# DeltaNet and Fourier mixing on one core: odd heads' tokens of batches 2 to 4 with their partition halves exchanged

## The chip, the cores and the metric

The kernel runs on one core of a Trainium2 chip. The metric is the device time of one execution in microseconds (us); lower is better. Engines are named as in the profile: PE is the matrix engine (PEld its weight loads), DVE the vector engine, ACT the scalar engine, POOL the third elementwise engine, SP the queue that issues most transfers. Matrix results land in eight banks of an accumulator memory, PSUM, from where DVE or ACT must copy them out.

## The reference, cut to what matters

Four batches, eight heads, 768 tokens, head size 48. First a recurrence per head, then a block that mixes over all tokens and features by Fourier transforms, and a two-layer network.

```python
for t in range(S):                      # DeltaNet, per batch and head
    y[:, :, t] = np.einsum('bhd,bhde->bhe', q[:, :, t], state)
    v_old = np.einsum('bhde,bhd->bhe', state, kt)
    state = state + bt * np.einsum('bhd,bhe->bhde', kt, vt - v_old)
...
x = y.transpose(0, 2, 1, 3).reshape(B, S, H * D)
mixed = np.real(np.fft.fft(np.fft.fft(x, axis=1), axis=2))
u = x + mixed
un = (u - mu) / np.sqrt(var + 1e-06)
out = u + np.maximum(un @ w_ch1, 0.0) @ w_ch2
```

Keys are divided by their norms first.

## The kernel before, in words

The 768 tokens of a batch are cut into six units of 128 tokens, so there are units 0 to 23; a unit stands on the 128 partitions as two chunks `c` of 64 tokens. Heads are taken in four pairs `j`, with `s` = 0 for the even and 1 for the odd head of a pair. Within a chunk the recurrence is solved as a triangular system (products of keys in `gram`, an inverse built on DVE in `invert`, lines 859 and 864, and joined by small products in `quarters`); from chunk to chunk only the state `st` (48 x 48 for each head) is carried.

For a unit of batches 2 to 4 (units 6 to 23) these steps follow each other:

- `load`: k, q and v by one transfer each, or two of 121 and 7 rows for units 6 to 13 (line 399, queue of SP).
- `ahead`: the inverse times v gives U (tile `ut`, buffers `u`), copied out of PSUM in three parts; the inverse times k gives the factor for the state.
- `step(z, c)`: sixteen small products of the state (PE, `f1`: U's correction and the outputs' first part); two subtractions on 64 partitions from U, one for the even and one for the odd heads (DVE, line 1174); two copies of outputs to `x` (ACT or DVE); eight products of keys and U (PE, `f2`); one addition to the state on 128 partitions (DVE, line 1203). The next `f1` waits for that state.
- `outputs`: sixteen products, and four additions on 64 partitions to `x` (DVE, line 1240), or two copies and two additions in the first unit of a batch.

The odd head's result of chunk `c` comes out of PE on the other 64 partitions than the even head's, and this is why the subtractions and additions go by 64 partitions. Batch 1 (units 0 to 5) takes another path (`chain0`, `outputs0`), which the change leaves alone.

After the last unit of a batch come its mixing (`folds` on DVE, `seq6` and `feat` on PE) and the network (`mlp`, `mlpw`: groups of four or six wide matrix products, first layer and second layer in turn). Their products stand between the steps of the next batch's recurrence.

Each instruction belongs to an operation `P.op`; the order of all operations, the engine of those that two engines can do, the PSUM banks, and a few products that only keep PE running (`fill`, lines 2057 and 2063) are written out as the text ORDER. Each engine takes its instructions in that order and waits at each for what it reads.

Of the kernel before, what the change touches and what calls it, by code (L numbers as in the profile page):

```python
# [53 lines left out]
APBAAAWAZAZAXv8AABAaAaAOBA+A+AIBAFBAGBAJBA9A9AHBANBACBA7A7ADBAMDA8A8AQDALDAEDAKDARATAYAbBCAeDEAdBAcC  # L54
AUFASAfBAgBAhGHH-H-AVCxCxAwAiDXDXBSABIIIIAjBPCDH3H3Alv+EAkBQCC6C6AmBTCv+FDFDFBRCAvA-ECBUCBCAFBACBVDB
BBCv-EBDCBWBkA1Axv-EAyBECAzBFCAA5BXA0A2v-EAtBZBGBYAnv-EA3BvBHv-EBwBaBJv-EBzAoBIBev-EB0BKArv-EB3BOBjv
-EBhBbv-EDgBhBcv-EBMIAIAv-EIHIHB4v-EA6BlC5AtB7ApBpv-EBmDODOAqwAFB8BNDCBUBnBLB-BoBfIQIQCACyBACDBiH4H4
BtDYGHCEBdv-EBqDfDfC0CDaCC7FCIXIXCHCzCBrDGDACIDZCBsDhHBBxCLDHCv-EByCMDICIPIPB1CPDbGDDjCB2CQDiCB5C1AB
CTC8CB6C9CCUv-EB9DdCIoIoCXB+C3Cv-ECYCBAuv-ECbIJCCIYIYCcDkHFCFA4AsCGBgCfDPCDCJCgC2CDuDuCKv-EIBCjCkCNC
+BACnDDCIfIfv-ECOv-ECov-EDQCv-EDNBLCpC-Cv-EILDJCBCRDRCDyInInv-ED1CD2BESDzCCSD3DDcCD0BCrDLCEXGETCDwDw  # L60
D4CIDv-ECVCqD5BEYCEVCH5DSDGDWBvCWv-EEWCD7EUCCZv-EDACD6CaDlCD8EZBCdIRD9H6EAADTCCeEbD+CEav+EChEcD-CCiE
dEDCICEBCEgHClEeBEECCmECCv-EH8EhCCsEFDH7v-EBuIKEGCv-ECtH9DmCEHCv-EEkCv-EEJCCuFCCv-EDKCEICv-EFACEjBEN
BAEfCH+IZEKFCE+FqIwIwFBCDEBEiCv-EIxIxEPCE-BFDDFuBELCIEIyIyEOCFvHCwITIvIvIFEQFFECEMCv-ECvFwCERCElDFtC
DUCFFCIGFrCGZCEwEnCFsBEoCGWI6I6DMEmCFxHEpCI5I5GbGDVEyCI7I7GYCHFCEqDBFHI8I8GXCFzEzCHCFyDoDoC4IzExHAHD
BEsCFGErCFIHHCI0I1E0FJIMGcCFMBHICHEBI2E1Cv-EGaBDpBFNCGdDFLCFQBI3EtGCF0FPCF1I9E5GfNmFPGeEuBFOCF4DIgIg
ISE6CI4EvCE7CE2DqCFKBJIJIHGBIUFRBJGJGI+E8JHJHIaF3CFUBIVwAEJEJEE3CF8BFTCGgJFJFF5BE9CHJGF2CF7BJDJDF6BI
NFcIhFVBHLF9DHKFSCFfBI-FeBFWGBF+BIbGhFdAHJAF-CE4BJBGACFYBFgGBCHMGjCGkCFXBIjFhBGCBDObHNGmCHPBFlHOCIiG
DCHQGFnBFmCGECDBJJFoIOFZBDFpCJCHTCv-EJcJcGnCGIFaCJbJbIpGlBIkv-EJdJdFbCHRBGKCFiJaJaGLCJKHUCGoBJQJQGiC
DrBGJAHIrNnE4IcNoFdDsBFkCGMJLJeJeJMGpCHSBNlE5GNCJNGFDGJZJZGqBFjBGrCGRNpGXGHBGsCHVBGGCIlNsE9GSBGTCGtC
v-EN-GqHWBGUHXCGOHZCJOGVBIdJmJmHYBGQBJfG0DvDvGPBGuCBNxFxG2CIWJnJnJhG1GDOAGHGvBGwCG3CImNyNyJSJSG4DnJo  # L70
JoHaABIqG5CDtDtGxCHJRJRHbBG9GyBGzCHcCIsG6DeG+CG-CItHAG8BG7COBABHBBKqHgKpv-EHjCODBHdCHHiCIuHhDGRZODHe
COCCOdHfBIeHkONHhHmJPJPKrHlBRNFiKtHpOOKrKsHnCNzBAHoCJqJqKwHrCHqBKxN0CKyHsKzOECHHtCRQHqKuN1CK2NrFQHxK
vDxDxK6HuBFJTJlJlHyBK5RMRMK0HvCN2ADJUHzCJpJpHwCJVK1RRK0K9H0LAK3N5LLEGJgH1CK4H2CLBOFK7N4JiRnOFN7K8OIN
qDeLELUBFK-K+RPHzLCLIRYKtLDLHR0N4LMLGLFRSRSLJJWRULULVLKJrOHJXN3N8OJN6LNJsN9JYLWLOCLSBJjLRBJzJzOGLQCR
1OGRaADLaBLXCwACOKRbCLdGCJkLPCRcCN+J-J-LbCOPHAOMLeOLJ0J0LmEDLgJxJxORCLfJ+J+LhOQCLvFCJ9J9JuLTCLiJyJyL
nLcCOSGAKAKALpLZCLoNvFgLYCLjJtLqRdHDJ7J7LkJ8J8LrOXJvLwLlOTL4EBLsOURjReMTLtRhOVRiMUCLuOYL5MKDGMWMVCL7
OWL6J1MXBOaMBCAJwMYCKBJ2MbEKLKLOZKKKKKDKCLyKMKMLxNwF6KEMCJ3OcNuFWKFKHKHMLMZBRmK3KJKJSCKIKIKGOeOfJ4Kh
# [11 lines left out]
MtYtYOTfDBRJYXNREYLYYYMRISPCYbTgRLTiYZThBYaRKYWYfGDT7HAYgBYhCTkCTjCUABT8DGTlYPTmBCYNT9CUBBNSCYiFDTnT
pToCYdT+CUXATqCYjTrEYmYnTtBGUYCTsT-CUCCATvTwTuUZEYqUGCNTHBUECUbBYoUdCYlUaCUcBYkUFUDTxU2UHDYpUeEFYcUI  # L90
YsUfACUkCUiCUJGDUgCNWUhCbiUhU3YuX9StUKYvX+SuUNCYwULCbcYfYxUMUjCU4U6YyNUEU5U9YzY1Y6U+UOANVCUQCGUPbdYw
U7UlDFbvYxUTY7bjEAUUURNXGU8blCUSUoUnCbkCUmVAU-Y8VDUqCVBVGbmADY9beU-UrVCNkNkUsECbpNZVFUwCY+brY-NYCUvZ
# [153 lines left out]
def kernel(  # L246
# [895 lines left out]
    def step(z, c, pr):  # L1142
# [8 lines left out]
        for i in range(k):  # L1151
# [36 lines left out]
            if n == 2 * NT - 1:  # L1188
                continue
# [907 lines left out]
```

## Time and profile before

| what | value |
|---|---|
| three runs, median | 633.43 us (630.84 to 637.3) |
| the profiled execution | 633.59 us, span of its instructions 631.8 us |
| granted PE clock, mean | 0.997 |
| PE instructions | 9694 matmul records for 5078 products of the program |
| DVE, ACT instructions | 1597, 890 |

A row of the groups reads: line, engine, operation, result <- operands, shape, count | busy us, mean ns of one | idle time of the engine just before, and what ended it. One small product leaves two records on PE, so a count of 1056 is 528 products. PE's busy time counts the modelled ends of products, so a short wait can lie under it unseen.

### The profile page before, as it was taken

The page shows a single profiled execution, that of the slowest core. Times are in us where ns is not written, and L with a number is a line of the kernel's source. Part 1 is how long each engine was busy: PE and PEld are TensorE (multiplying, and loading weights), DVE is VectorE, ACT ScalarE, POOL GpSimd, SP SyncE. Part 2 cuts the span into 40 slices and gives each one's busy share as a digit, 9 for nine tenths or more (in the row PEclk, how much of TensorE's full clock was granted, in tenths as well). Part 3 has the DMA queues.
Part 4 walks back from the last instruction along what each step waited for, and adds up shares of the span by engine and source line. Part 5 has one row for each costly group of instructions (what it writes and reads, how often), then busy time and mean ns, then how long its engine had stood idle before and what let it go on. Part 6 is the DMA issues. An engine that isn't in the chain of part 4 may idle for free.

```text
span 631.8 us, 22692 instructions
## 1 busy us (share of the span) xinstructions
PE 613.7 (97%) x9694; PEld 508.3 (80%) x9694; DVE 530.8 (84%) x1597; ACT 287.5 (46%) x890; POOL 31.0 (5%) x37
## 2 busy tenths in 40 slices
PE   9999899999999899999999999999999999999997
PEld 8788798777678678877787778867778789999997
DVE  6999799999997799999957999999865867777563
ACT  6999657633556435447443334553631112222111
POOL 2013302210000000000000000000000000000000
PEclk9999899999999999999999999999999999999999
DMA  8842654500014151000330330000000000010100
GB/s 191 225 136 74 161 132 113 141 1 1 3 29 104 38 124 22 2 1 3 66 78 23 87 71 1 2 28 2 4 3 2 2 1 1 1 51 1 51 26 25
DMA packets 85442, 31.99 MB, mean 51 GB/s; under 512 B 75996, under 2 KB 80829, under 8 KB 85341
## 3 DMA queue, kind: packets, MB, share of 16 engines
q1 hardware_dynamic: 85149, 30.31, 19.6%
q8 instruction: 76, 1.25, 0.8%
q10 hardware_dynamic: 192, 0.23, 0.2%
q14 instruction: 25, 0.20, 0.1%
HBM read 25.82 MB, written 4.72 MB: 48 GB/s over the span
## 4 chain that ended last, share of the span: by engine, by line
PE 46%; DVE 3%; issue 1%; ACT 0%; DVEq 0%
PE pp L348 44%; PE pp L351 1%; DVE tmp L859 1%; DVE rr L864 1%; DVE gd L876 0%; DVE st L1203 0%; DVE u L1174 0%; ACT us L357 0%; DVE x L1787 0%; DVE x L359 0%; DVE rr L873 0%; DVE x L1240 0%; DVE us L1728 0%; DVE us L1580 0%; DVE u L1787 0%
## 5 line engine op out<-in xcount | busy, mean ns | idle before, releaser
L348 PE MATMUL pp<-R,w 128*128 128x256 f32 (+1 forms) x832 | 180.6, 366 | 0.2 <-ACT R L357 0.2
L348 PEld LDWEIGHTS pp<-R,w 128*128 128x128 f32 x832 | 146.2, 190 | 20.3 <-ACT R L357 0.4
L348 PE MATMUL pp<-w,R 128*128 128x384 f32 x384 | 133.9, 493 | 0.0
L357 ACT ACTIVATE us<-pp 32x128 f32<-32x128 f32 (+3 forms) x218 | 71.3, 352 | 78.0 <-PE pp L348 47.9
L348 PEld LDWEIGHTS pp<-w,R 128*128 128x128 f32 x384 | 70.2, 190 | 40.6
L348 PE MATMUL pp<-us 64*64 64x64 f32 (+4 forms) x2784 | 69.3, 230 | 0.7 <-ACT u L357 0.4
L348 PEld LDWEIGHTS pp<-us 64*64 64x64 f32 (+2 forms) x2784 | 58.6, 131 | 8.7 <-issue 3.6
L859 DVE TENSOR_TENSOR tmp<-rr 128x108 f32<-128x108 f32 (+12 forms) x180 | 58.8, 333 | 2.6
L864 DVE TENSOR_TENSOR rr<-rr,tmp 128x30 f32<-128x30 f32 (+11 forms) x180 | 57.8, 327 | 2.8
L348 PEld LDWEIGHTS pp<-u,us 64*64 64x64 f32 (+1 forms) x1472 | 38.0, 132 | 15.3 <-issue 6.0
L1519 ACT ACTIVATE R<-pp 128x512 f32<-128x512 f32 x46 | 27.1, 594 | 49.3 <-PE pp L348 43.2
L348 PE MATMUL pp<-u,us 64*48 64x48 f32 (+2 forms) x1472 | 44.2, 218 | 4.5 <-ACT u L357 2.8
L1694 DVE TENSOR_TENSOR us<-us,pp 128x256 f32<-128x256 f32 x64 | 26.5, 417 | 14.1 <-ACT us L357 9.1
L357 ACT ACTIVATE us<-us,nr 128x48 f32<-128x48 f32 x144 | 34.0, 322 | 0.4 <-DVE nr L666 0.4
L348 PE MATMUL pp<-st,us 48*64 48x48 f32 (+1 forms) x1232 | 28.7, 223 | 5.3 <-issue 2.5
L357 ACT ACTIVATE x<-pp 64x192 f32<-64x192 f32 (+1 forms) x57 | 17.9, 325 | 33.3 <-PE pp L348 25.6
L348 PEld LDWEIGHTS pp<-st,us 48*64 48x64 f32 x1232 | 24.1, 136 | 9.4 <-issue 5.8
L357 ACT ACTIVATE R<-pp 128x384 f32<-128x384 f32 (+7 forms) x48 | 19.2, 408 | 24.3 <-PE pp L351 12.8
L1174 DVE TENSOR_TENSOR u<-u,pp 64x192 f32<-64x192 f32 x66 | 22.2, 349 | 9.0 <-PE pp L348 6.0
L357 ACT ACTIVATE u<-pp 64x192 f32<-64x192 f32 (+1 forms) x59 | 19.1, 326 | 20.1 <-PE pp L348 15.6
L348 PE MATMUL pp<-us,gd 128*128 128x192 f32 x144 | 27.5, 326 | 0.0
L1240 DVE TENSOR_TENSOR x<-x,pp 64x192 f32<-64x192 f32 x66 | 23.2, 351 | 4.0 <-PE pp L348 1.3
(183 smaller groups left out, 1008.0 us busy)
## 6 DMA issues: line engine op xcount, KB each, us to landing
out_dram<-x SPq DMA_DIRECT2D x11, 384.0 KB
us<-in_k_dram SPq DMA_DIRECT2D x16, 192.0 KB
us<-in_q_dram SPq DMA_DIRECT2D x16, 192.0 KB
us<-in_v_dram SPq DMA_DIRECT2D x16, 192.0 KB
x<-in_moe_w_ch_dram SPq DMA_DIRECT2D x11, 242.0 KB
R<-in_moe_w_ch_dram SPq DMA_DIRECT2D x8, 256.0 KB
us<-in_k_dram SPq DMA_DIRECT2D x8, 181.5 KB
us<-in_q_dram SPq DMA_DIRECT2D x8, 181.5 KB
```

The lines of the kernel that those rows point to most:

```text
L348: I(nc.tensor.matmul(o, lhsT=lhsT, rhs=rhs, start=start, stop=stop, skip_group_check=True))
L351: I(nc.tensor.matmul(o, lhsT=src, rhs=ident[p0:p0 + n, p0:p0 + n], is_transpose=True, start=start, stop=True, skip_group_check=True))
L357: I(nc.scalar.activation(o, i, ACT.Copy, **({} if scale is None else {"scale": scale})))
L859: I(eng(e).tensor_tensor(T_, R[:, :, j + 1:32, j:j + 1].broadcast_to([128, ns, n, j]), R[:, :, j:j + 1, 0:j].broadcast_to([128, ns, n, j]) ...
L864: I(eng(e).tensor_tensor(R[:, :, j + 1:32, 0:j], R[:, :, j + 1:32, 0:j], T_, op=ALU.add))
L1174: I(nc.vector.tensor_tensor(U[:, s], U[:, s], psum(b1[s])[a, s0:s1].rearrange("p (j d) -> p j d", d=D), op=ALU.subtract))
L1240: I(nc.vector.tensor_tensor(w, w, v, op=ALU.add))
L1519: I(nc.scalar.activation(o, s, ACT.Relu))
L1694: vec(256, lambda e: I(nc.vector.tensor_tensor(o, i0(), i1(), op=ALU.add)), [], [aH] + list(wr), pr - P.ev, use=n)
```

## The change

For batches 2 to 4 the tokens of the odd heads are loaded with the two 64-partition halves of a unit exchanged (`swapped`, new). Then the odd head's result of chunk `c` comes out on the same 64 partitions as it will be used with, in the other half than the even head's, and one instruction on 128 partitions does for both. U is kept by chunk, 192 columns for each, no longer by head. The products' number and sizes stay; which half of the rows and columns of PE a product uses, and which bank it fills, changes. The decay column `bcol` of the odd heads is exchanged too, by two more copies at the start (`odd`).

```diff
+    def swapped(z, what, pr):
+        for y in what:
...
+            for s in range(2):
+                parts = ((0, 64), (64, 128)) if s else ((0, ROW), (ROW, 128)) if z.u < 14 else ((0, 128),)
+                for x0, x1 in parts:
+                    r0 = z.T * 128 + (x0 ^ 64 if s else x0)
+                    o = dst[x0:x1, s, :, 0:D]
+                    dma(o, src[s, r0:r0 + x1 - x0], [tuple(w)], pr, kb=100 * (x1 - x0) / 128)
 # load
+        if z.b:
+            return swapped(z, what, pr)
 # ahead
-                    a, x = slice(64 * c, 64 * c + 64), 64 * (c ^ s)
-                    mm(psum(b2[s])[x:x + 64, D * j:D * j + D], z.TT[a, 2 * j + s, :],
+                    a = slice(64 * (c ^ s), 64 * (c ^ s) + 64)
+                    mm(psum(b2[c])[64 * s:64 * s + 64, D * j:D * j + D], z.TT[a, 2 * j + s, :],
                        z.V[a, 2 * j + s, :], j == 0)
...
-            copy(e, us[:, 0], psum(b2[0])[:, 0:W].rearrange("p (j d) -> p j d", d=D))
+        P.op({"ACT": 0.23, "DVE": 0.27}, lambda e: copy(e, z.ut[:, 0:W], psum(b2[0])[:, 0:W]), [], [A(z.ut, 0, W)],
 # step
-                            for q, y in ((1, 64 * c), (0, 64 - 64 * c)):
-                                mm(psum(b1[s])[y:y + 64, D * j:D * j + D], z.QK[r, q, c, j, :],
-                                   so[r, D * j:D * j + D], j == js[0])
+                            o = half(s) if y else half(1 - s)
+                            mm(psum(b1[y])[o, D * j:D * j + D], z.QK[r, y, c ^ s, j, :],
+                               so[r, D * j:D * j + D], j == 0)
...
-                for s in range(2):
-                    def g1(e, s=s, s0=s0, s1=s1, b1=b1):
-                        I(nc.vector.tensor_tensor(
-                            U[:, s], U[:, s],
-                            psum(b1[s])[a, s0:s1].rearrange("p (j d) -> p j d", d=D),
-                            op=ALU.subtract))
+            vec(W, lambda e: I(nc.vector.tensor_tensor(u, u, psum(b1[1])[:, 0:W], op=ALU.subtract)),
+                [], [aU], pr - P.ev - 5, use=[b1[1]])
...
-                        mm(t[64 * s:64 * s + D, D * j:D * j + D], z.K[a, 2 * j + s, 0:D],
-                           z.U[a, 2 * j + s, :], j == js[0])
+                    mm(t[64 * s:64 * s + D, D * j:D * j + D], z.K[half(s), 2 * j + s, 0:D],
+                       u[half(s), D * j:D * j + D], j == 0)
 # outputs
-        for c in range(2):
-            for s in range(2):
-                y = 64 * (c ^ s)
+        for s in range(2):
+            for i, (p0, p1) in enumerate(((0, 64), (64, 128)) if z.T == 0 else ((0, 128),)):
...
+                        I(nc.vector.tensor_tensor(w, w, v, op=ALU.add))
 # ORDER, first row
-APBAAAWAZAZAXv8AABAaAaAOBA+A+AIBAFBAGBAJBA9A9AHBANBACBA7A7ADBAMDA8A8AQDALDAEDAKDARATAYAbBCAeDEAdBAcC
+APBABAaAbAbAZwrAAAAcAcACDAKBA-A-AIBAYAEBBABAA9A9A+A+AQDAODAGDAFDALDAdBCAJDAUDARAfCANDAeCAgEFAHDICICA
```

(`half(s)` is the half `c ^ s` of the 128 partitions.) The whole ORDER is another. Three places show what it moves.

On DVE, in the steps of unit 10 (batch 2; `u_84` is its U, `st` the states, `x_97` the outputs, `pm`, `eo` and `rr` belong to the folds and the inverse of later work), before:

```order
L1174 TENSOR_TENSOR u_84<-u_84,pp_61 64x4x48
L1174 TENSOR_TENSOR u_84<-u_84,pp_63 64x4x48
L1240 TENSOR_TENSOR x_97<-x_97,pp_67 64x4x48
L1265 TENSOR_TENSOR pm_99<-x_97 128x384
L592 SCALAR_TENSOR_TENSOR gd<-us_77,pack,lo_86 128x4x32
L592 SCALAR_TENSOR_TENSOR gd<-us_76,pack,lo_87 128x4x32
L1203 TENSOR_TENSOR st_93<-st_92,pp_64 128x192
```

and in the changed program:

```order
L1181 TENSOR_TENSOR u_84<-u_84,pp_66 128x192
L362 COPY x_97<-pp_68 64x4x48
L680 MEMSET rr 128x32
L1203 TENSOR_TENSOR st_93<-st_92,pp_66 128x192
L1263 COPY eo_100<-pm_99 128x2x2
L362 COPY us_80<-pp_65 128x4x64
L1257 TENSOR_TENSOR eo_100<-pm_99 128x2x191
L1181 TENSOR_TENSOR u_84<-u_84,pp_68 128x192
```

The two subtractions have become one on 128 partitions, two other instructions and no longer four stand between it and the state's addition, and DVE takes copies to `x` here.

On PE, the end of unit 10's second step (`st` with `us_79` is `f1`, `u_84` with `us_79` in 48x48 is `f2`, `w` and `R` with 128 rows are network products), before:

```order
L348 MATMUL pp_67<-st_93,us_79 64x48 x2
L348 MATMUL pp_64<-st_93,us_79 64x48 x2
L348 MATMUL pp_68<-w_73,R_81 128x384
L348 MATMUL pp_62<-w_73,R_81 128x384
L348 MATMUL pp_68<-w_73,R_81 128x384
L348 MATMUL pp_62<-w_73,R_81 128x384
L348 MATMUL pp_65<-R_81,w_72 128x256 x6
L348 MATMUL pp_61<-u_84,us_79 48x48 x8
```

and in the changed program, where `pack` is a product of `fill` that computes nothing used:

```order
L351 MATMUL pp_68<-st_93,us_79 64x48 x2
L351 MATMUL pp_61<-st_93,us_79 64x48 x2
L2062 MATMUL pp_62<-pack 64x256 x2
L351 MATMUL pp_66<-u_84,us_79 48x48 x8
L351 MATMUL pp_65<-u_84,us_79 64x48
```

Two groups of network products that stood between `f1` and `f2` are gone from there, and a short filler stands in their place.

On PE, just ahead of that, the first step's `f2` and the second step's `f1` (changed program; `us_80` is the preparation of unit 11):

```order
L351 MATMUL pp_62<-us_80 64x64
L351 MATMUL pp_65<-us_80 64x64
L351 MATMUL pp_62<-us_80 64x64
L351 MATMUL pp_66<-u_84,us_79 48x48 x8
L351 MATMUL pp_68<-st_93,us_79 64x48 x2
```

Here `f1` follows `f2` with nothing between, where before the preparation of unit 11 stood between them.

Counted over the whole program, PE has 5078 products before and after, among them 112 of `fill` in both. DVE goes from 1597 to 1563 instructions, ACT from 890 to 837, POOL from 37 to 42, SP from 186 transfers to 294. Groups of network products between the first `quarters` and the first `seq6` of a batch: 15 in both for batch 2, 22 then 20 for batch 3, 25 then 22 for batch 4.

More of the change, by code (lines that the diff above doesn't have):

```diff
@@ L89 @@
[L89 to L92, printed above, removed]
-AUpCZBbnUtboZCbqVEZDVHbsUxCGUuBZEbwFAU1b8bsUzNcbfbpbxCU0YBYpUybyCX-M-VIVJZFVMbzDEZGVKVLb9GFZHVQVNNaC
@@ L1160, in f1 @@
+        aU = A(z.ut, W * c, W * c + W)
+        half = lambda s: slice(64 * (c ^ s), 64 * (c ^ s) + 64)
+        if n > 0:
+            b1 = two("attn")
+            def f1(e):
+                for j in range(NJ):
+                    for y in (1, 0):
                         for s in range(2):
                             r = slice(64 * s, 64 * s + D)
[L1162 to L1164 removed]
@@ new lines, in step, with f2, g2 @@
+        if n == 2 * NT - 1:
+            return
+        b2 = Bank("attn")
+        def f2(e):
+            t = psum(b2)
+            for j in range(NJ):
+                for s in range(2):
+                    mm(t[64 * s:64 * s + D, D * j:D * j + D], z.K[half(s), 2 * j + s, 0:D],
+                       u[half(s), D * j:D * j + D], j == 0)
+        def g2(e):
+            if n == 0:
+                copy(e, sn, psum(b2)[:, 0:W])
+            else:
+                I(nc.vector.tensor_tensor(sn, so, psum(b2)[:, 0:W], op=ALU.add))
```

279 lines of the change are left out of this document (130 added, 149 removed).

## The prediction

> **What bounds the kernel now.** The page's first two parts come first: busy time by engine, and the 40 slices of the span.
>
> ```profile
> PE 613.7 (97%) x9694; PEld 508.3 (80%) x9694; DVE 530.8 (84%) x1597; ACT 287.5 (46%) x890; POOL 31.0 (5%) x37
> PE   9999899999999899999999999999999999999997
> DVE  6999799999997799999957999999865867777563
> ACT  6999657633556435447443334553631112222111
> ```
>
> PE is busy nearly throughout, DVE nearly throughout until about slice 28 (440 us), ACT less than half. The second view is busy time by stretch, cut where the work changes: batch 1's recurrence, its mixing, the stretch in which the recurrences of batches 2 to 4 run (160 to 500 us), and the network alone.
>
> ```profile
> core 0: us, PE busy (x) PEld busy (x) DVE busy (x) ACT busy (x) POOL busy (x), PEclk, DMA share, GB/s
> 0.00:88.70 88.70, 82.60 (x2289) 71.26 (x2289) 78.12 (x269) 70.71 (x218) 18.25 (x24) 0.98 0.60 152
> 88.70:160.00 71.30, 70.83 (x496) 56.37 (x494) 69.41 (x206) 35.95 (x107) 11.50 (x10) 1.00 0.30 71
> 160.00:500.00 340.00, 332.22 (x6053) 258.34 (x6052) 296.05 (x841) 153.85 (x491) 1.23 (x4) 1.00 0.14 32
> 500.00:631.80 131.80, 128.04 (x863) 122.31 (x861) 87.19 (x284) 26.98 (x75) 0.00 (x0) 1.00 0.05 19
> ```
>
> What the change saves lies in the third row: there PE stands visibly idle for 340.0 - 332.2 = 7.8 us and DVE for 44, while ACT has 186 to spare. The last row has no recurrence in it, and the chain that ended last shows it as one run of PE, which the change cannot shorten:
>
> ```profile
> 489.43 43.72 PE pp L348 x298
> 571.47 54.63 PE pp L348 x368
> ```
>
> The third view is who waited for whom, for PE:
>
> ```profile
> PE pp L348 <- ACT u L357: 3.2, 4, 1.9
> PE pp L348 <- issue: 2.9, 4, 1.0
> PE pp L348 <- DVE u L1174: 1.4, 2, 0.8
> PE pp L348 <- ACT x L357: 0.9, 2, 0.6
> PE pp L348 <- DVE st L1203: 0.7, 3, 0.4
> ```
>
> PE hardly ever waits for the subtractions (1.4 us, twice) or the state's additions (0.7 us, three times). So the kernel is bound by PE's own work, and vector work counts only where it holds up a step.
>
> **The vector work that goes.** The groups by line, engine and shape:
>
> ```profile
> L1174 DVE TENSOR_TENSOR u<-u,pp 64x192 f32<-64x192 f32 x66 | 22.2, 349 | 9.0 <-PE pp L348 6.0 <-ACT R L1519 1.0 <-issue 0.6
> L1240 DVE TENSOR_TENSOR x<-x,pp 64x192 f32<-64x192 f32 x66 | 23.2, 351 | 4.0 <-PE pp L348 1.3 <-ACT x L357 1.3
> L1203 DVE TENSOR_TENSOR st<-st,pp 128x192 f32<-128x192 f32 x30 | 10.6, 352 | 14.7 <-PE pp L348 8.5 <-issue 4.3 <-ACT us L357 0.8
> L359 DVE COPY x<-pp 64x192 f32<-64x192 f32 x22 | 7.8, 354 | 1.1 <-PE pp L348 0.6
> L357 ACT ACTIVATE x<-pp 64x192 f32<-64x192 f32 x50 | 15.8, 324 | 30.3 <-PE pp L348 22.7 <-DVE u L1174 7.0
> ```
>
> The state's addition has 128 partitions and takes 352 ns, the subtraction has 64 and takes 349: partitions cost nothing, so each merged pair saves one whole instruction. There are 33 steps with a subtraction (11 for each of three batches): 66 become 33, and 33 x 0.349 = 11.5 us go. Of 66 additions to `x`, two go in each of 15 units (the first unit of a batch keeps its four instructions): 30 x 0.351 = 10.5 us. Together 22.0 us.
>
> But the order does not leave that on DVE. ACT's instructions fall by 53, DVE's by 34, though all 63 that are removed stood on DVE: copies that ACT did have gone over to it. At ACT's 0.32 us, 53 are some 17 us; DVE keeps the rest, about 5 us, of its 530.8. In the busy stretch DVE so stays near 290 of 340 us, and the relief is ACT's, which was not short of time. The two copies for the odd heads' decay (at most 2 x 0.35 us) fall in DVE's first slice, which is 6 tenths busy; I take them as nothing, 0.7 us if that cover is gone.
>
> **The step itself.** The timeline at a place where little covers the step, unit 8's first, without most rows of other work between:
>
> ```profile
> 192.92 0.68 PE L348 MATMUL pp<-st,us 48*64 48x48 f32 x32
> ...
> 193.42 1.07 PE L348 MATMUL pp<-us 48*64 48x128 f32 x32
> ...
> 193.70 0.61 DVE L1174 TENSOR_TENSOR u<-u,pp 64x192 f32<-64x192 f32 x2 [0.29 <-PE pp L348]
> ...
> 194.45 0.56 PE L348 MATMUL pp<-u,us 64*48 64x48 f32 x16
> ...
> 195.11 0.35 DVE L1203 TENSOR_TENSOR st<-st,pp 128x192 f32<-128x192 f32 x1 [0.80 <-ACT x L357]
> ...
> 195.61 0.68 PE L348 MATMUL pp<-st,us 48*64 48x48 f32 x32 [0.59 <-ACT x L357]
> ```
>
> The 1.07 us are `gram` of unit 12; between `f2` and the next `f1` stands nothing. From one `f1` to the next are 2.69 us. One subtraction in place of two makes 0.61 into 0.35: a step becomes 0.26 us shorter. That counts only where PE then waits. By the waits above these are seven places (two for `u`, three for `st`, two for `x`): 7 x 0.26 = 1.8 us; the most that can go is all of those waits and no more, 1.4 + 0.9 + 0.7 = 3.0 us, as DVE and ACT queues ahead of the step become shorter too. I take 3.0, because the steps that wait stand behind queues, as the 0.80 us ahead of 195.11 shows. What is late next is the network product behind, which needs nothing of the step.
>
> **PE's products.** Their number and sizes stay; their order over PE's halves changes. By shape:
>
> ```profile
> L348 PE MATMUL pp<-st,us 48*64 48x48 f32 x1056 | 23.2, 221 | 5.0 <-issue 2.5 <-DVE st L1203 0.7 <-ACT x L357 0.6
> L348 PE MATMUL pp<-u,us 64*48 64x48 f32 x528 | 18.3, 208 | 1.4 <-DVE u L1174 1.4
> L348 PE MATMUL pp<-u,us 64*64 64x48 f32 x576 | 13.4, 221 | 0.0
> L348 PE MATMUL pp<-us 64*64 64x48 f32 x576 | 12.9, 221 | 0.0
> L348 PE MATMUL pp<-st,R 48*64 48x64 f32 x176 | 8.4, 230 | 0.0
> ```
>
> Busy time by record: `f1` 23.2/1056 = 22.0 ns, `f2` 34.7, `outputs` 23.3, `ahead` 22.4. `f1`, `outputs` and `ahead` go through all four quarters (row half by column half) of PE in turn, before and after. `f2` uses two quarters that share a row half today, and two that lie across from each other after. If it then ran at `f1`'s pace, 528 x (34.7 - 22.0) = 6.7 us of PE would go. The one row with two quarters that lie across is the product of `st` and `R` in batch 1, and it takes 47.7 ns, for 64 columns in place of 48: scaled by columns 35.8. I take 0, by this row, and keep -6.7 for the range. The Trainium skill, TensorEngine Tiling (Array Packing), section Tiling Modes, says that tiles work independently and that different tiles can load weights and multiply in parallel; by that `f2` should gain, and the sum would be by 6.7 us lower. The trace agrees for four quarters in turn, not for two.
>
> **Transfers.** Bytes and the 192-byte rows stay, the number of transfers goes from 186 to 294.
>
> ```profile
> 300.77 0.37 SPq L399 DMA_DIRECT2D us<-in_q_dram  x1
> L1839 ACT ACTIVATE w<-x 128x512 f32<-128x512 f32 x9 | 6.1, 684 | 4.5 <-DMA x<-in_moe_w_ch_dram 2.6 <-DMA us<-in_k_dram 1.8
> ```
>
> At 0.37 us for an issue, 108 more are 40 us of SP's queue, spread over 400 us in which SP does nothing else. Where it is dense, up to 117 us, units 6 to 11 add 36 issues, 13 us, and behind them in the queue stand the network's weights, for whose arrival ACT waits already (4.5 us in the second row). From 160 us on DMA is 14% busy and hides it. I take 0, and 3 us for the range, if the weights come late.
>
> **The rest of the order.** The first 160 us are ordered anew with the same work, most of the 112 filler products among it. Nothing speaks for a sign; 3 us either way go into the range.
>
> **Sum.** Against the profiled 633.6 us, which stands 0.2 above the median of the runs: vector work beside PE 0, step -3.0, products 0, transfers 0, so 630.6. Forecast 630 us.
>
> **Rivals.** Within 1% (6.3 us) no change can be told.
>
> *Faster, 624 us:* every step counts, not seven. PE's busy time hides short waits, for its weight loads stood idle in the stretch more often than PE shows:
>
> ```profile
> PEld pp L348 <- issue: 16.1, 37, 1.1
> ```
>
> Then 33 x 0.26 = 8.6 us go, or the 6.7 of `f2` with the 3.0: 624 to 625. For it: that row, and 7.8 us of visible idle. Against it: "issue" is no wait for a vector result.
>
> *Slower, 643 us:* the new order trusts the shorter step and takes its cover away. In units 9 to 11 five steps have less than 1 us of products between `f2` and `f1` or `f1` and `f2`, as in unit 10 with a filler alone. A bare step takes 2.69 - 0.26 = 2.43 us, of which PE works 23.2/33 + 18.3/33 = 1.26; five idle steps are 5.9 us. In batches 3 and 4 five groups of network products leave the recurrence, and one is dear:
>
> ```profile
> L348 PE MATMUL pp<-w,R 128*128 128x384 f32 x384 | 133.9, 493 | 0.0
> ```
>
> 133.9/48 = 2.8 us a group, 14 us of cover; if half of it is missed, 7. Together +13 against the 3 gained: 643 to 644. It decides once each of the five bare steps shows over 1 us of idle PE. Against it: PE's total work is the same, so a group that is taken from here covers another wait elsewhere.
>
> *Slower, 651 us:* the two row halves of PE cannot fill one bank at once. Today each bank of `f1` and `outputs` is filled from one half; after the change from both. At the pace of one half (`f2`'s 34.7 ns) `f1` would cost 1056 x 12.7 = 13.4 us and `outputs` 576 x 11.4 = 6.6 us more: +20 - 3. Against it: `ahead` fills its banks from both halves already, at 22.4 ns. The Trainium skill, TensorEngine Tiling (Array Packing), section Restrictions and Gotchas, states that different row tiles cannot access the same PSUM bank simultaneously; the row of `ahead` does not agree.
>
> That the change doesn't do what it says is excluded by the order: the 128-partition instructions stand there.
>
> **Numbers.** Chances: within 1% 0.42; faster 0.30; covers gone 0.23; banks 0.05. So faster by over 1% 0.30, within 0.42, slower 0.28. The forecast's own range is 625 to 637 (the 3 us of transfers and of the first stretch, the unknown of the steps). Eight times in ten reaches from 619 (624 less the 3 of the first stretch and 2 of the steps) to 648 (643 with 3 for transfers and 2), and leaves out the banks and the far ends.
>
> **What would show it.** Right: 33 subtractions and 36 additions to `x`, each at 0.35 us on 128 partitions; ACT's busy time down by some 17 us, DVE's by some 5; `f2` at 34 ns a record, `f1` and `outputs` at 22 to 23; PE idle in the recurrences' stretch 4 to 6 us; the network's tail alone as long as now. Wrong: `f2` well under 30 ns (faster), idle of over 1 us at `f2` in units 9 to 11 (slower), `f1` over 30 ns a record (banks), or a first mixing that starts more than 3 us earlier or later than at 88.7 us, in which case the order of the first stretch, and not the change, made the time.

## The result, and the profile after

| | median us | runs | ratio to before, 95% interval |
|---|---|---|---|
| before | 632.78 | 6 | |
| changed | 640.99 (639.07 to 641.72) | 6 | 1.0122 [1.0085, 1.0159] |

The change made the kernel slower by 1.2%, 8.2 us. The profiled execution of the changed kernel took 640.02 us, its span 638.2; against the span of 631.8 before, that is 6.4 us, so the two profiles show most of the 8.2 and not all. First the page's busy time:

```profile
PE 616.2 (97%) x9694; PEld 509.8 (80%) x9694; DVE 522.3 (82%) x1563; ACT 268.2 (42%) x837; POOL 30.4 (5%) x42
```

The vector engines were relieved as forecast: DVE by 8.5 us, ACT by 19.3. The groups show the merged instructions at the price of the old ones, and the products at their old pace:

```profile
L1181 DVE TENSOR_TENSOR u<-u,pp 128x192 f32<-128x192 f32 x33 | 11.5, 350 | 12.5 <-PE pp L351 12.2
L1236 DVE TENSOR_TENSOR x<-x,pp 128x192 f32<-128x192 f32 x30 | 9.9, 347 | 0.7
L351 PE MATMUL pp<-st,us 48*64 48x48 f32 x1056 | 23.3, 221 | 2.1 <-issue 1.1 <-DVE eo L1263 0.5 <-DVE st L1203 0.2
L351 PE MATMUL pp<-u,us 64*48 64x48 f32 x528 | 18.5, 207 | 1.5 <-issue 1.3
L351 PE MATMUL pp<-u,us 64*64 64x48 f32 x576 | 13.1, 220 | 0.2 <-issue 0.2
```

Where the time went is read by cutting both spans at the first product of each batch's mixing (`tab` with `R`, which stands in the timeline of PE at these times):

```profile
88.69 1.06 PE L348 MATMUL pp<-tab,R 128*97 128x193 f32 x5
...
94.64 1.06 PE L351 MATMUL pp<-tab,R 128*97 128x193 f32 x5
```

Busy time in the five stretches between these cuts, before:

```profile
0.00:88.69 88.69, 82.59 (x2288) 71.25 (x2288) 78.11 (x269) 70.70 (x218) 18.25 (x24) 0.98 0.60 152
88.69:243.43 154.74, 149.84 (x2404) 117.28 (x2401) 143.71 (x412) 77.57 (x239) 12.10 (x11) 1.00 0.28 64
243.43:376.94 133.51, 132.54 (x2230) 102.92 (x2230) 118.25 (x342) 60.69 (x189) 0.62 (x2) 1.00 0.19 41
376.94:509.05 132.11, 129.72 (x1954) 101.34 (x1951) 112.33 (x316) 52.74 (x173) 0.00 (x0) 1.00 0.02 5
509.05:631.80 122.75, 118.99 (x827) 115.50 (x825) 78.36 (x261) 25.79 (x73) 0.00 (x0) 1.00 0.06 20
```

and in the changed kernel (columns as in the prediction's stretches):

```profile
0.00:94.64 94.64, 84.34 (x2280) 70.98 (x2280) 81.52 (x268) 73.11 (x220) 22.37 (x32) 1.00 0.64 157
94.64:248.18 153.54, 150.29 (x2380) 118.29 (x2378) 139.37 (x397) 67.73 (x211) 7.41 (x8) 1.00 0.26 55
248.18:382.46 134.28, 130.77 (x2256) 102.70 (x2254) 113.93 (x328) 58.89 (x197) 0.62 (x2) 1.00 0.19 41
382.46:515.22 132.76, 131.66 (x1963) 102.44 (x1959) 110.03 (x311) 41.22 (x135) 0.00 (x0) 1.00 0.02 5
515.22:638.20 122.98, 119.14 (x827) 115.42 (x826) 77.47 (x265) 27.28 (x75) 0.00 (x0) 0.99 0.06 20
```

The first stretch grew by 5.95 of the 6.4 us by which the spans differ, the four others together by 0.45. It holds batch 1, whose steps the change leaves alone, and PE does the same work in it: 2288 records and 2280, and the difference is fillers. Two further rows show the loads. PE now waits for tokens, which it did not do before; the three waits lie at 244, 362 and 377 us, far behind the first stretch:

```profile
PE pp L354 <- DMA us<-in_q_dram: 2.2, 3, 0.8
```

and SP's queue is fuller: from 100 to 123 us it issues for 19.7 of 23 us, where it was 12.6 before. Some of its rows in the changed kernel at 107 us (start, duration, line, result):

```profile
107.09 0.60 SPq L402 DMA_DIRECT2D us<-in_q_dram  x1
...
108.61 0.60 SPq L402 DMA_DIRECT2D us<-in_v_dram  x1
109.26 0.55 SPq L402 DMA_DIRECT2D x<-in_moe_w_ch_dram  x1
109.86 0.60 SPq L402 DMA_DIRECT2D us<-in_v_dram  x1
```

The 64-row transfers of the odd heads take 0.60 us or more to issue (median 0.61); the whole load that the prediction quoted took 0.37. Over the program SP's issues grew from 97.3 to 160.6 us, added up over all of them.

So three theories stood. **Order:** the new order of the first stretch costs 6 us by itself. **Cut loads:** the 294 transfers in place of 186 cost it. **Steps:** the merged steps and their places on PE cost what they save. The experiments combine the two programs' operations with the two programs' orders; loads, steps and first stretch are then exchanged one by one.

### The profile page after: what moved, and what is told of

It is laid out like the page before. It is cut to its first block, busy times and chain, and to the rows that moved or that the text cites. A ratio compares the mean times of both kernels' runs of the same rounds, so it can differ in the third digit from the quotient of the medians.

```text
span 638.2 us, 22753 instructions
## 1 busy us (share of the span) xinstructions
PE 616.2 (97%) x9694; PEld 509.8 (80%) x9694; DVE 522.3 (82%) x1563; ACT 268.2 (42%) x837; POOL 30.4 (5%) x42
## 4 chain that ended last, share of the span: by engine, by line
PE 76%; DVE 11%; SPq 3%; DMA 3%; ACT 3%; issue 2%; DVEq 0%; ACTq 0%
PE pp L351 73%; SPq L402 3%; PE pp L354 2%; DMA x<-in_moe_w_ch_dram 2%; DVE R L1257 1%; ACT us L360 1%; DMA us<-in_q_dram 1%; DVE tmp L768 1%; DVE w L774 1%; DVE w L1850 1%; PE pp L2056 1%; DVE eo L1257 1%; DVE tmp L878 1%; DMA ws<-in_moe_w_ch_dram 1%; DVE rr L797 0%
## 5 line engine op out<-in xcount | busy, mean ns | idle before, releaser
L360 ACT ACTIVATE us<-pp 128x256 f32<-128x256 f32 (+3 forms) x205 | 67.2, 342 | 76.1 <-PE pp L351 54.2
L351 PE MATMUL pp<-us 64*64 64x64 f32 (+4 forms) x2784 | 72.8, 230 | 3.1 <-issue 1.7
L878 DVE TENSOR_TENSOR tmp<-rr 128x108 f32<-128x108 f32 (+11 forms) x180 | 59.6, 336 | 2.8
L883 DVE TENSOR_TENSOR rr<-rr,tmp 128x108 f32<-128x108 f32 (+11 forms) x180 | 57.7, 326 | 2.6
L1511 ACT ACTIVATE R<-pp 128x512 f32<-128x512 f32 x37 | 21.9, 593 | 69.4 <-PE pp L351 69.4
L351 PE MATMUL pp<-u,us 64*64 64x48 f32 (+2 forms) x1472 | 44.2, 216 | 4.0 <-issue 2.1
L360 ACT ACTIVATE us<-us,nr 128x48 f32<-128x48 f32 x120 | 28.5, 322 | 9.0 <-DVE nr L685 8.4
L360 ACT ACTIVATE x<-pp 64x192 f32<-64x192 f32 (+1 forms) x60 | 19.5, 324 | 20.1 <-PE pp L351 17.5
L2062 PE MATMUL pp<-pack 64*64 64x256 f32 (+1 forms) x186 | 27.6, 384 | 0.0
L351 PEld LDWEIGHTS pp<-ft,R 97*128 97x128 f32 (+1 forms) x192 | 23.8, 191 | 2.8 <-ACT R L360 0.3
```

Source lines behind the costliest of these rows:

```text
L351: I(nc.tensor.matmul(o, lhsT=lhsT, rhs=rhs, start=start, stop=stop, skip_group_check=True))
L360: I(nc.scalar.activation(o, i, ACT.Copy, **({} if scale is None else {"scale": scale})))
L878: I(eng(e).tensor_tensor(T_, R[:, :, j + 1:32, j:j + 1].broadcast_to([128, ns, n, j]), R[:, :, j:j + 1, 0:j].broadcast_to([128, ns, n, j]) ...
L883: I(eng(e).tensor_tensor(R[:, :, j + 1:32, 0:j], R[:, :, j + 1:32, 0:j], T_, op=ALU.add))
L1511: I(nc.scalar.activation(o, s, ACT.Relu))
L2062: I(nc.tensor.matmul(pst[bank][x, 0:256], lhsT=w[x, 0:128 // tiles], rhs=w[x, 0:256], start=True, stop=True, skip_group_check=True))
```

## The experiments

**The two orders, whole or in part.** Four kernels change only the text ORDER, of which the first row is shown.

`e1_new_old_head`, against the changed kernel:

```diff
-APBABAaAbAbAZwrAAAAcAcACDAKBA-A-AIBAYAEBBABAA9A9A+A+AQDAODAG...
+APBAAAYAbAbAZwrAABAcAcAOBBABAAIBAFBAGBAJBA-A-AHBANBACBA9A9AD...
...
```

> The changed program; its operations up to the first mixing stand in the order that the program before had for them, the rest as in the changed program. If the order of the first stretch makes the loss: the first mixing starts at 88 to 90 us instead of 94.6, and the time is 634 to 636 us, within 0.5% of before. If the loads in halves or the products' new places make it: it stays at 639 to 642 us, with the first mixing still after 93 us or the later batches' stretches longer.

657.33 us (1.0377 [1.0331, 1.0422]). The first mixing came at 89.6 us, so the old order does restore the first stretch, also with cut loads. But where the two orders were joined, PE stood still:

```profile
PE pp L351 <- ACT x L360: 14.9, 1, 14.9
```

It waits for a copy to `x` by ACT, and ACT, which takes its instructions in order, had waited for transfers ahead of that copy, at work on the network's weights (from 85 to 107 us):

```profile
ACT w L1831 <- DMA ws<-in_moe_w_ch_dram: 6.6, 2, 6.0
ACT w L1831 <- DMA us<-in_q_dram: 6.0, 1, 6.0
```

The total therefore measures the join of two orders and says nothing on the change.

`e2_old_new_head`, against before:

```diff
-APBAAAWAZAZAXv8AABAaAaAOBA+A+AIBAFBAGBAJBA9A9AHBANBACBA7A7AD...
+APBABAYAZAZAXv8AAAAaAaACDAKBA9A9AIBAWAEBA+A+A7A7A8A8AQDAODAG...
...
```

> The program before; its operations up to the first mixing stand in the changed program's order. If the order of the first stretch makes the loss: first mixing at 94 to 95 us and 638 to 640 us, though no load is halved and no step is changed. If the change's own operations make it: 632 to 634 us, as before.

642.62 us (1.0168 [1.0124, 1.0213]), a little above the expected 640, first mixing at 94.8 us. The old program, without a single cut load, becomes as slow in the first stretch as the changed one. The theory of the order holds that far. What moves there is seen on SP (before with a minus, the new order with a plus):

```order
 L399 DMA x_97<-in_moe_w_ch_dram 128x512
+L399 DMA R_98<-in_moe_w_ch_dram 128x512 x2
 L399 DMA us_75<-in_q_dram 128x8x48
-L399 DMA us_79<-in_q_dram 128x8x48
-L399 DMA x_97<-in_moe_w_ch_dram 128x512
 L399 DMA ws<-in_moe_w_ch_dram 128x512
 L399 DMA us_76<-in_q_dram 128x8x48
+L399 DMA ws<-in_moe_w_ch_dram 128x512
+L399 DMA x_97<-in_moe_w_ch_dram 128x512
 L399 DMA us_77<-in_q_dram 128x8x48
```

The network's weights (`in_moe`) go ahead of q and v of batch 1.

`e3_new_old_order`, against the changed kernel:

```diff
-APBABAaAbAbAZwrAAAAcAcACDAKBA-A-AIBAYAEBBABAA9A9A+A+AQDAODAG...
+APBAAAYAbAbAZwrAABAcAcAOBBABAAIBAFBAGBAJBA-A-AHBANBACBA9A9AD...
...
```

> The changed program with all its operations in the order of before (a merged instruction stands where the first of the two stood). It shows the change without the new order. By the forecast's step term: 3 us under before, 629 to 631 us. If vector time at the steps is hidden altogether: 632 to 634. If the operations themselves are dearer (halved loads, banks filled from both row halves): 638 or more.

650.91 us (1.0264 [1.0205, 1.0324]): every expectation but the dearest fell. In the old order the changed operations lose 18 us.

`e4_old_new_order`, against before:

```diff
-APBAAAWAZAZAXv8AABAaAaAOBA+A+AIBAFBAGBAJBA9A9AHBANBACBA7A7AD...
+APBABAYAZAZAXv8AAAAaAaACDAKBA9A9AIBAWAEBA+A+A7A7A8A8AQDAODAG...
...
```

> The program before with all its operations in the changed program's order (two subtractions stand where the merged one stood). If the order makes the loss: 638 to 642 us, and up to 644 if the steps without cover need the merged instruction. If the change's own operations make it: 632 to 635.

662.67 us (1.0460 [1.0405, 1.0515]), far above all of it. The new first stretch alone cost the same program 10 of these 30 us (`e2`); the rest says that the new order needs the merged instructions.

**The loads alone.** `e5_old_parted`, against before:

```diff
+    def parted(z, what, pr):
...
+                parts = ((0, 64), (64, 128)) if s else ((0, ROW), (ROW, 128)) if z.u < 14 else ((0, 128),)
+                for x0, x1 in parts:
+                    r0 = z.T * 128 + x0
...
+        if z.b:
+            return parted(z, what, pr)
```

> The program before, in its own order, with each load of units 6 to 23 cut into the same 3 or 4 transfers as in the changed program (294 in place of 186, same bytes, rows not exchanged). If the transfers made the 18 us by which the changed program in the old order was slower: 645 to 651 us, PE waiting for k and q of units 6 to 11, mixing of batch 2 some 11 us later. If the merged steps and banks made them: 632 to 635.

660.76 us (1.0417 [1.0370, 1.0464]), 10 above the upper expectation. Cutting the loads, and nothing else, costs the old kernel 27 us. Not all of it is waiting: PE's granted clock over the span was 0.97 to 0.99 in all six runs. In the profile PE's waits for tokens of 1.2, 1.5 and 1.0 us end at 236.5, 346.0 and 376.0 us, and at 237.5, 346.8 and 377.5 the clock falls to half for 3.4 us each.

`e6_new_whole_old_order`, against the kernel of `e3`, and `e7_new_whole`, against the changed one, have the same edit:

```diff
-        if z.b:
-            return swapped(z, what, pr)
-        for x0, x1 in ((0, 128),):
+        for x0, x1 in ((0, ROW), (ROW, 128)) if 6 <= z.u < 14 else ((0, 128),):
```

> The changed program in the order of before, with whole loads as before (186 transfers; the odd heads' halves are then not exchanged, so their values are not the reference's). What is left of the change are merged steps, merged additions and the new places on PE. If the transfers made the 18 us: 628 to 634 us, and how far under 633 it comes is what the merged vector work is worth (forecast: 3 us). If the steps and banks made them: 645 to 651.

633.31 us (0.9988 [0.9965, 1.0010]): the 18 us of `e3` were the cut loads. The merged vector work, in the old order, is worth 0.1%, not told apart from nothing.

> The changed program in its own order with whole loads (186 transfers, halves not exchanged). If the order of the first stretch makes the loss whatever the loads are: 638 to 641 us, first mixing at 94 to 95. If the cut loads hold the changed program back within its own order too: 630 to 636.

634.69 us (1.0013 [0.9987, 1.0039]), 6.3 below the changed kernel, though its profiled first mixing came only at 98.6 us. The gain lies behind it, from mixing to mixing:

```profile
98.57:249.38 150.81, 149.00 (x2380) 117.58 (x2378) 137.84 (x390) 68.43 (x212) 7.44 (x8) 1.00 0.22 52
249.38:380.97 131.59, 130.09 (x2255) 102.38 (x2253) 115.05 (x332) 58.86 (x197) 0.62 (x2) 1.00 0.19 41
380.97:512.58 131.61, 131.41 (x1962) 102.32 (x1959) 109.99 (x311) 41.27 (x135) 0.00 (x0) 1.00 0.02 5
```

The changed kernel has 153.54, 134.28 and 132.76 there, before 154.74, 133.51 and 132.11. So the new order with the merged steps does gain some 6 us there, and the cut loads eat them.

`e8_old_new_load_order`, against before (ORDER alone, SP's rows of the first stretch):

```diff
-APBAAAWAZAZAXv8AABAaAaAOBA+A+AIBAFBAGBAJBA9A9AHBANBACBA7A7AD...
+APBAAAWAZAZAXv8AABAaAaAOBA9A9AIBAFBAGBAJBA+A+A7A7AHBA8A8ANBA...
...
```

> The program before in its own order, but the loads of the first stretch go into the queue in the order of the changed program (the network's weights ahead of q and v of units 0 to 5). If the order of the loads delays the first stretch: first mixing at 93 to 96 us and 638 to 642 us. If the order of the vector and matrix work does: first mixing at 88 to 90 and 632 to 635.

647.84 us (1.0205 [1.0169, 1.0242]), first mixing at 100.9 us. The order of the loads does delay the first stretch, and by more than the expected bound. PE waits 3.9 us at once for q there, and its granted clock in that stretch is 0.95, where it was 0.98 before. The rest of the old order did not go along with the loads; whether that is why was not tried.

**Who issues.** `e9_new_pool_queue`, against the changed kernel:

```diff
-            after = take(2) if o.kb and e == "SP" else i
+            after = take(2) if o.kb and e in ("SP", "POOL") else i
...
+                        q="POOL" if s else "SP")
```

> The changed program in its own order; the 108 transfers of 64 rows (the odd heads' halves) are issued by POOL, which is idle, and no longer by SP. The same transfers arrive in the same places. If the price of the cut loads is SP's issue time (108 at 0.60 us, 65 us of its queue): 633 to 636 us, as with whole loads (634.7). If it is their number on the DMA engines or their late arrival whoever issues them: 640 or more.

(The first edited line only gives POOL's transfers places of their own in ORDER.) 636.83 us (1.0065 [1.0043, 1.0087]): 4.2 of the 6.3 us come back, so neither end of the expectation holds. From mixing to mixing the profile has 150.64, 131.71 and 132.97 us, in sum 5.3 less than the changed kernel and 1.3 more than `e7`. With the same 294 transfers, most of the gain behind the first mixing is back, which points to the time of SP's queue and not to the transfers themselves.

`e10_new_even_whole`, against the changed kernel:

```diff
-                parts = ((0, 64), (64, 128)) if s else ((0, ROW), (ROW, 128)) if z.u < 14 else ((0, 128),)
+                parts = ((0, 64), (64, 128)) if s else ((0, 128),)
```

> The changed program in its own order; the even heads' tokens of units 6 to 13 come in one transfer of 128 rows and no longer in two of 121 and 7, so 24 transfers less on SP at 0.3 us each. If every issue in the dense stretch counts: 637 to 640 us. If only the 64-row transfers count: 640 to 642.

643.01 us (1.0159 [1.0123, 1.0195]), above both expectations: 24 issues fewer, 4.5 us of SP's queue in all (156.1 in place of 160.6), bring nothing. Not every issue has a price.

`e13_new_act_queue`, against the changed kernel:

```diff
+                        q="ACT" if s else "SP")
```

> The changed program in its own order; the 108 transfers of 64 rows are issued by ACT, which is busy 42% of the span, and no longer by SP. If SP's issue time is the price and ACT's spare time hides it: 633 to 637 us, with no stretched DVE instructions as from POOL. If 65 us of issues (0.60 each) on ACT hold its copies up: 642 or more.

640.41 us (1.0116 [1.0090, 1.0142]), between the two expectations: with ACT as issuer nothing that can be measured comes back.

**First stretch and loads, two by two.** `e11_new_whole_old_head` has the edit of `e7` and, as `e12`, `e14` and `e15`, this beginning of ORDER, kept up to unit 6's first `f2`, where nothing is dense:

```diff
-APBABAaAbAbAZwrAAAAcAcACDAKBA-A-AIBAYAEBBABAA9A9A+A+AQDAODAG...
+APBAAAYAbAbAZu-AABAcAcAOBBABAAIBAFBAGBAJBA-A-AHBANBACBA9A9AD...
...
```

> The changed program with whole loads (186 transfers, halves not exchanged, so the odd heads' values are not the reference's); up to the second product of unit 6's first step it stands in the order of before, from there in the changed order. If the order of the first stretch costs 6 to 8 us by itself and the changed order gains behind it: first mixing at 88 to 91 and 625 to 629 us. If the changed order's gain behind the first stretch only makes up for what it puts off there: 632 to 635.

626.20 us (0.9906 [0.9875, 0.9937]), as the first expectation has it. All its stretches with a recurrence are shorter than before's 88.69, 154.74, 133.51 and 132.11. Of the 2.1 us of the first row, 1.3 are PE's busy time on the same work, at a granted clock of 1.00 where it was 0.98 before, and so not the change's:

```profile
0.00:86.61 86.61, 81.26 (x2289) 69.79 (x2289) 78.87 (x272) 70.41 (x218) 18.24 (x24) 1.00 0.61 155
86.61:238.34 151.73, 148.95 (x2376) 117.47 (x2373) 136.59 (x392) 73.44 (x228) 11.69 (x11) 1.00 0.28 66
238.34:369.72 131.38, 130.16 (x2256) 102.54 (x2254) 114.92 (x332) 58.78 (x197) 0.62 (x2) 1.00 0.19 42
369.72:501.34 131.62, 131.42 (x1962) 102.41 (x1959) 110.01 (x311) 41.24 (x135) 0.00 (x0) 1.00 0.02 5
```

`e15_new_old_head_late` is the same with the cut loads:

```diff
-        for x0, x1 in ((0, ROW), (ROW, 128)) if 6 <= z.u < 14 else ((0, 128),):
+        if z.b:
+            return swapped(z, what, pr)
+        for x0, x1 in ((0, 128),):
```

> The changed program, complete, all transfers on SP, with the order of before up to the second product of unit 6's first step. If the order of the first stretch and the transfers are two separate costs: 633 to 635 us (641 less 6 to 8). If the changed order of the first stretch is what the cut loads need (the weights go first because SP is full behind): 640 or more, with unit 6's second step at 180 us or later in place of 175.

643.71 us (1.0160 [1.0123, 1.0196]): the second expectation, with unit 6's second step at 191 us. The first mixing is early, and the profile loses 13 us right behind it:

```profile
0.00:90.17 90.17, 81.38 (x2289) 70.27 (x2289) 79.08 (x273) 70.76 (x218) 18.22 (x24) 0.98 0.58 146
90.17:254.87 164.70, 157.99 (x2376) 125.18 (x2374) 136.90 (x394) 73.81 (x228) 11.68 (x11) 0.95 0.28 62
...
PE pp L354 <- DMA us<-in_q_dram: 4.4, 5, 2.3
...
PE pp L354 <- DMA us<-in_k_dram: 1.6, 2, 1.3
```

The waits for q and k are the smaller part of it. The longest for k lies at 10 us, in the first stretch; the longest for q ends at 100.94 us, and 2 us later PE's granted clock falls to half, for 17.1 us in which PE is never idle:

```profile
100.94 0.46 PE L354 MATMUL pp<-pack,us 64*128 64x64 f32 x8 [2.31 <-DMA us<-in_q_dram]
103.00:120.10 17.10, 17.10 (x133) 15.94 (x132) 11.10 (x29) 9.97 (x28) 2.80 (x3) 0.50 0.40 106
```

Against `e11`, PE idles 6.71 us in the second row and not 2.78, and it is busy for 157.99 us and not 148.95 with the same 2376 records: 9 of the 13 us show as longer busy time, and the half clock can explain up to 8.5 of them (half of 17.1). That the wait brought on the slow clock is likely from its place, here and in `e5`, but was not tried. The kernel is slow without it too: the four runs with a mean clock of 0.995 or more took 639.11 to 644.41 us.

With `e7` and the changed kernel this is a table of the two causes (medians, us):

| | whole loads | cut loads |
|---|---|---|
| old order up to unit 6's first step | 626.20 | 643.71 |
| new order | 634.69 | 640.99 |

The cut loads cost 17.5 us under the old order and 6.3 under the new one. The new first stretch costs 8.5 us where the loads are whole, and saves 2.7 where they are cut. So the two are not separate costs. The reading that fits is that the new order pays in the first stretch, by sending the weights early, for a queue that is full behind.

By this table the way from before to the changed kernel is -6.6 us (merged steps and the new order behind the first stretch, `e11`), +8.5 (the new first stretch, `e7`) and +6.3 (the cut loads): the 8.2 us that were measured.

`e12_new_pool_old_head`, against `e15`:

```diff
+                        q="POOL" if s else "SP")
```

> The changed program, complete, with the 64-row transfers issued by POOL and the order of before up to the second product of unit 6's first step. If both causes are removed: 625 to 630 us, faster than both programs. If the transfers cost as much from POOL: 638 or more.

637.56 us (1.0063 [1.0030, 1.0097]).

`e14_new_act_old_head`, against `e15`:

```diff
+                        q="ACT" if s else "SP")
```

> The changed program, complete, with the 64-row transfers issued by ACT and the order of before up to the second product of unit 6's first step. If both causes add up as they did with whole loads (626.2): 627 to 631 us, faster than both programs. If ACT is too full in the first 165 us: 636 or more.

637.27 us (1.0088 [1.0060, 1.0117]). Both miss their first expectation: another queue takes 6 us off `e15`, not 17. What is left lies behind the first mixing: from there to the fourth mixing the profiles take 423.6 and 421.8 us, `e11` 414.7. Its cause stays open. In `e12` a vector instruction of the first stretch grew while POOL worked and issued; the same one in `e11` and in `e12`:

```profile
68.48 1.08 DVE L1844 SCALAR_TENSOR_TENSOR w<-ws,w 128x512 int32<-128x512 int32 x1
...
69.00 3.59 DVE L1851 SCALAR_TENSOR_TENSOR w<-ws,w 128x512 int32<-128x512 int32 x1
```

**What the gain rests on.** `e17_new_whole_split`, against `e11`:

```diff
-            vec(W, lambda e: I(nc.vector.tensor_tensor(u, u, psum(b1[1])[:, 0:W], op=ALU.subtract)),
+            def g1(e, b1=b1):
+                for p in (slice(0, 64), slice(64, 128)):
+                    I(nc.vector.tensor_tensor(u[p], u[p], psum(b1[1])[p, 0:W], op=ALU.subtract))
...
-                        I(nc.vector.tensor_tensor(w, w, v, op=ALU.add))
+                        for y in range(0, p1 - p0, 64):
+                            I(nc.vector.tensor_tensor(w[y:y + 64], w[y:y + 64], v[y:y + 64], op=ALU.add))
```

> As the run with whole loads and the old first stretch (626.2 us; the odd heads' values are not the reference's), but each merged subtraction and addition is two instructions on 64 partitions again: 63 more on DVE, 22 us of its time, in the same order. If the gain behind the first stretch rests on the saved vector time: 634 us or more, at least 8 above. If it rests on where the products stand and the vector work is hidden, as the forecast had it for all but seven steps: 627 to 630.

644.17 us (1.0183 [1.0151, 1.0215]): 18.0 us above `e11` for 22 us of vector instructions. In the new order most of this vector time is on the path. The stretches with merged steps are 16.8 us longer than `e11`'s 151.73, 131.38 and 131.62, at the same granted clock:

```profile
86.66:245.87 159.21, 151.33 (x2375) 118.24 (x2373) 146.35 (x413) 73.98 (x229) 11.88 (x11) 1.00 0.26 62
245.87:380.39 134.52, 131.82 (x2255) 102.88 (x2255) 123.20 (x351) 58.56 (x198) 0.62 (x2) 1.00 0.18 41
380.39:518.23 137.84, 133.45 (x1959) 103.03 (x1959) 119.83 (x334) 41.31 (x135) 0.00 (x0) 1.00 0.02 5
```

The waits of PE for `u` and `st`, 1.4 and 0.7 us in the kernel before, are 2.8 and 1.9; the rest does not show as single waits of PE:

```profile
PE pp L347 <- DVE u L1177: 2.8, 5, 1.5
...
PE pp L347 <- DVE R L1254: 2.3, 2, 2.0
PE pp L347 <- DVE st L1199: 1.9, 4, 0.9
```

**The exchange without cut loads.** `e16_copied_exchange`, against `e11`; `sc` is a second copy of q, k and v in the chip's memory, from which the units of batches 2 to 4 are loaded whole:

```diff
+    def exchange(bb):
+        for y, src in (("k", k), ("q", q), ("v", v)):
+            ins, outs = (x[bb].rearrange("(j s) (t c p) d -> s c t j (p d)", s=2, c=2, p=64) for x in (src, sc[y]))
+            for h in range(2):
+                dma(outs[1, 1 - h], ins[1, h], [("sc" + y, h, h + 1, bb, bb + 1)], 0, kb=295)
...
+            dma(outs[0], ins[0], [("sc" + y, 2, 3, bb, bb + 1)], 0, kb=590)
...
+        K, Q, V = (sc[y] if z.b else x for y, x in (("k", k), ("q", q), ("v", v)))
```

> The changed program, complete and exact: 27 large transfers copy q, k and v of batches 2 to 4 inside the chip's memory, the odd heads with their 64-row halves exchanged, and the units then load whole tokens from that copy (186 loads as before; the order is that of the run with whole loads and the old first stretch). If only the cut loads hold the change back: 626 to 630 us, faster than both programs. If the 3.5 MB of batch 2's copy between 30 and 60 us delay the network's weights or unit 6's k: first mixing after 90 us, or unit 6's second step after 178 us, and 632 or more.

630.78 us (0.9968 [0.9944, 0.9992]), between the two expectations: faster than before by 0.3%, just clear of its interval, faster than the changed kernel by 10 us, and 4.6 us above `e11`. Behind the first mixing, at 89.6 us, its stretches are `e11`'s again:

```profile
89.56:241.91 152.35, 149.70 (x2376) 117.56 (x2373) 136.80 (x392) 73.30 (x228) 11.87 (x11) 1.00 0.40 112
241.91:373.49 131.58, 129.89 (x2255) 102.25 (x2254) 114.91 (x332) 58.85 (x197) 0.62 (x2) 1.00 0.19 41
373.49:505.21 131.72, 131.53 (x1963) 102.24 (x1959) 110.03 (x311) 41.28 (x135) 0.00 (x0) 1.00 0.02 5
```

`e18_copied_exchange_2`, against `e16` (ORDER alone; the rows of SP's queue that move, `sc_v` from further down):

```diff
 L399 DMA sc_k<-in_k_dram 16x4x2304
+L399 DMA sc_q<-in_q_dram 6x4x3072 x2
+L399 DMA sc_q<-in_q_dram 16x4x2304
 L399 DMA ws<-in_moe_w_ch_dram 7x512
...
 L399 DMA us_80<-in_v_dram 128x8x48
-L399 DMA sc_q<-in_q_dram 6x4x3072 x2
-L399 DMA sc_q<-in_q_dram 16x4x2304
+L399 DMA sc_v<-in_v_dram 6x4x3072 x2
+L399 DMA sc_v<-in_v_dram 16x4x2304
```

> The complete kernel with the exchange by copies, with batch 2's copy of q moved from 46 to 34 us and that of v from 56 to 48 us, into the stretch in which the transfer engines stand nearly idle (35 to 40 us). If the 3 us that it lost ahead of the first mixing came from copies beside the network's weights: 627 to 629 us. If the copies' volume itself delays: 630 to 632 as before.

630.57 us (0.9960 [0.9936, 0.9985]): the place of the copies is not what is left; whether it is their volume was not tried apart.

## Why the prediction was wrong, step by step

- **What bounds the kernel, the vector work, the products:** held for the old order. DVE lost 8.5 us (5 forecast), ACT 19.3 (17). Of the 36 additions to `x` that were forecast on 128 partitions, 30 are, and 6 stay on 64. `f2` runs at 18.5/528 = 35.0 ns a record, as before (34.7), though its two quarters now lie across: the value taken (0, not -6.7) was right. The Trainium skill, TensorEngine Tiling (Array Packing), section Tiling Modes, says that different tiles work in parallel; in these two quarters it does not show. `f1` (22.1 ns) and `outputs` (22.7) fill their banks from both row halves without loss, so the rival of the banks fell. The Trainium skill, TensorEngine Tiling (Array Packing), section Restrictions and Gotchas, says that different row tiles cannot access one PSUM bank at once; these runs show no cost of it.
- **The step, -3.0 us:** its mechanism was right for the old order and wrong for the new. With the loads whole, the merged work brings 0.1% in the old order (`e6`), 0.7 us of the 3.0 and not told apart from nothing. With the new order behind the first stretch it brings 0.9% (`e11`), and without the merged instructions that same order is 18 us slower (`e17`). The sum counted the waits of the old order as if the new one would keep its cover; by `e17` the new one spends that cover, and by `e11` it comes out 6.6 us ahead of the kernel before.
- **Transfers, "I take 0, and 3 us for the range":** this step failed. It priced an issue at 0.37 us and let DMA's low share hide it. The 64-row issues take 0.60 or more, SP's issues grew by 63 us and not 40, and others stand behind them in the same queue: the network's weights up to 120 us, and tokens for which PE then waits. Measured in one order, the cut loads cost 6.3 us under the new first stretch and 17.5 under the old one; each under the better of the two, 14.8 (640.99 - 626.20). The Trainium skill, DMA: Bandwidth & Descriptors, section Rules for kernel authors, advises against two transfers to disjoint partition halves and for one of 128 partitions. `e5` and `e15` agree, with 27 and 17.5 us, slow clock included.
- **The rest of the order, "3 us either way":** this term was too small as well. The first stretch grew by 5.95 us in the profiles, and the new one costs 8.5 us where the loads are whole (`e7` against `e11`). The prediction's last sentence, that a late first mixing would be the order's doing "and not the change", drew the line in the wrong place. `e2` shows that the order makes it; `e15` against `e11` shows that with cut loads the old order is no better.
- **Covers gone, 643 us:** near the measured time by luck. With the loads whole, the stretches that were to grow are shorter than before (`e7`), and in the changed kernel PE's idle time from first to second mixing is 3.25 us after (153.54 - 150.29) and 4.90 before (154.74 - 149.84), so the bare steps of units 9 to 11 cost nothing that shows.

Not settled: how much of the 14.8 us is SP's issue time and how much the transfers themselves. Under the new first stretch POOL as issuer gave back 4.2 of 6.3 us, which speaks for SP's queue; ACT gave back nothing, 24 fewer issues on SP nothing, and under the old first stretch neither POOL nor ACT gave back more than 6.4 of 17.5. How much of the 17.5 is the slow clock is open too.

## What to carry to other kernels

A change of layout is paid for where the data comes in: count its transfers, price each shape by a row of its own, and ask what stands behind it in the same queue, before counting the instructions that it saves. An order that was planned for one set of operations is a part of the program: the saved vector time was worth 0.7 us in the old order and 18 in the new one, so a change and its order have to be tested crosswise. Where a stretch that the change does not touch grows, exchange that stretch alone, and then once more with the suspected cause removed, before calling it chance. And where a stretch is long although PE is busy, read the granted clock and the number of records beside the waits.

## What was unexpected in the hardware

A transfer of 64 rows took 0.60 us or more to issue, in all 108 places and from SP, ACT and POOL alike; in the same queue 128 rows took 0.37 at best, 121 rows 0.29 and 7 rows 0.27. In these rows the price of an issue follows neither the bytes nor the number of rows; what makes 64 rows dear was not tried. PE's granted clock fell to half three times for 3.4 us in `e5` and once for 17.1 us in `e15`, each time about 1 to 2 us after a wait of PE for tokens of 1.0 to 2.3 us. While POOL issued transfers and worked beside DVE, one vector instruction took 3.59 us in place of 1.08. And 27 large transfers that copy 10.6 MB (q, k and v of three batches, 24 heads of 147 KB for each) cost the kernel 4.6 us (630.78 - 626.20) and 19.5 us of issues, where loads with 108 small transfers for half of these bytes, 71 us of issues in the same queue of SP, cost 6.3 to 17.5.
